# Feed-forward gradients with the hidden index as adjacent rows of w_down per partition, and products that contract the four batch rows

## The chip, the cores and the metric

The kernel runs on one core of a Trainium2 chip. The metric is the device time of one execution in microseconds (us). Each kernel was executed several times; the text gives medians, and beside them ratios to the kernel before. A program on one core also has faster and slower executions. "Clock" is the TensorE clock that the throttle granted, as a share of full speed.

## The reference, cut to what matters

The reference computes one decode step of a parallel attention and feed-forward block, and all its gradients.

```python
# B = 4 batch rows, S = 1, D = 512, F = 1792; 32 query heads, 8 KV heads, Sk = 4096, Dh = 128, bf16
def _A_ref(x, k_cache, v_cache, wq, wo):     # attention over the last W = 1024 keys
    ...
def _B_ref(x, w_gate, w_up, w_down):
    return (_gelu(x @ w_gate) * (x @ w_up)) @ w_down

xn = _layernorm(x)
out = x + _A_ref(xn, ...) + _B_ref(xn, ...)
# returned: out, and the gradients of x, k_cache, v_cache, wq, wo, w_gate, w_up, w_down
```

The gradients of the caches are zero outside the last 1024 keys, so the kernel also stores about 50 MB of zeros. The gradients of the three feed-forward weights are outer products summed over only four batch rows.

## The kernel before

Four parts matter. First, w_down is loaded so that hidden index f = c*128 + p: partition p holds the rows p, 128+p and so on, in packets of 1 KB.

```python
for c0 in range(0, NF, NF // 2):                       # NF = 14
    nc.sync.dma_start(out=wd_sb[:, c0:c0 + NF // 2, :],
                      in_=B_w_down[c0 * P:(c0 + NF // 2) * P, :].rearrange("(c p) n -> p c n", p=P))
```

Second, the feed-forward reads its weights in columns that lie side by side, and its masks are made on GpSimd.

```python
nc.tensor.matmul(h_ps[:, fc, :], lhsT=wsb[:, c, fc * P:(fc + 1) * P], rhs=xnT[:, c, :], ...)   # hg, hu
...
for src, dst in ((dy_b, dym), (xn_b, xnm)):
    for i in range(rep):
        nc.gpsimd.tensor_scalar(out=dst[:, i, :], in0=src[:], scalar1=msk_i[:, i:i + 1], ...)
```

Third, the weight gradients. The activations are turned into rows, four blocks of 128 hidden units in 4 rows per batch row; a product takes all 128 partitions, and the mask leaves four that are not zero. They run in the background of attention: each "tick" of the attention code starts one.

```python
def piece_d(f4, i, n, held):                           # gradient of w_down, 14 of these
    mps = ps_w.tile([P, D], FP32, name="dwd_ps", tag="w")
    nc.tensor.matmul(mps[:], lhsT=a_r[:, f4, :], rhs=dym[:, i, :], start=True, stop=True)
    ...
def piece_g(s_r, og, c, i, held):                      # gradients of w_gate and w_up, 32 of these
    n = (NF - i + 3) // 4                              # 4 or 3 blocks: 512 or 384 columns
    mps = ps_w.tile([P, NF4, P], FP32, name="dwg_ps", tag="w")
    nc.tensor.matmul(mps[:, 0:n, :].rearrange("p f d -> p (f d)"), lhsT=xnm[:, i, c:D:ND],
                     rhs=s_r[:, 0:n, :].rearrange("p f d -> p (f d)"), start=True, stop=True)
    evac(held["osb"][:, 0:n, i, :], mps[:, 0:n, :], n * P)
```

Fourth, attention runs in four steps t. Each step's gradients of V and K go through staging tiles, of which there are three; zeros are queued by ScalarE at fixed places (`zeros(4 if t >= NT - 2 else 0)` is one).

## Time and profile before

| | before |
|---|---|
| median of the first three runs | 284.48 us |
| span of the profiled run | 281.7 us |
| mean granted clock | 0.896 |
| TensorE busy | 210.1 us, 75% |
| DMA | 112.15 MB, mean 398 GB/s |

In a table of windows the columns are: stretch, its length, busy us (and instructions) of TensorE's matmuls, TensorE's weight loads, VectorE, ScalarE and GpSimd, then granted clock, DMA share, GB/s.

### The profile page before, as it was taken

The page shows a single profiled execution, that of the slowest core. Times are in us where ns is not written, and L with a number is a line of the kernel's source. Part 1 is how long each engine was busy: PE and PEld are TensorE (multiplying, and loading weights), DVE is VectorE, ACT ScalarE, POOL GpSimd, SP SyncE. Part 2 cuts the span into 40 slices and gives each one's busy share as a digit, 9 for nine tenths or more (in the row PEclk, how much of TensorE's full clock was granted, in tenths as well). Part 3 has the DMA queues.
Part 4 walks back from the last instruction along what each step waited for, and adds up shares of the span by engine and source line. Part 5 has one row for each costly group of instructions (what it writes and reads, how often), then busy time and mean ns, then how long its engine had stood idle before and what let it go on. Part 6 is the DMA issues. An engine that isn't in the chain of part 4 may idle for free.

```text
span 281.7 us, 7190 instructions
## 1 busy us (share of the span) xinstructions
PE 210.1 (75%) x3132; PEld 135.9 (48%) x3132; DVE 158.7 (56%) x336; ACT 115.6 (41%) x214; POOL 56.0 (20%) x56
## 2 busy tenths in 40 slices
PE   1968976968769699967793399786963996878950
PEld 0856854634536465534461265454641654526520
DVE  6945754626467457645672137547651465367691
ACT  1421743344535146535421335435502563571540
POOL 3890003400200633020024060110050201002000
PEclk9975999979988989999999559979995999799795
DMA  7999999999999999999999969999999779999995
GB/s 236 445 398 426 423 405 413 408 418 419 422 427 426 420 425 417 425 422 425 428 420 409 406 202 347 425 426 426 416 427 429 318 301 409 428 427 423 419 416 221
DMA packets 19407, 112.15 MB, mean 398 GB/s; under 512 B 1440, under 2 KB 5040, under 8 KB 10416
## 3 DMA queue, kind: packets, MB, share of 16 engines
q10 hardware_dynamic: 4384, 50.34, 42.4%
q1 hardware_dynamic: 12304, 44.58, 39.1%
q0 software_dynamic: 2688, 16.78, 15.1%
q8 instruction: 24, 0.39, 0.5%
q14 instruction: 7, 0.06, 0.0%
HBM read 30.68 MB, written 81.01 MB: 396 GB/s over the span
## 4 chain that ended last, share of the span: by engine, by line
PE 45%; DMA 27%; DVE 16%; ACT 4%; issue 3%; POOL 2%; ACTq 0%; DVEq 0%; SPq 0%
DMA out_dram<-stg_dv 18%; PE T_ps L399 10%; PE kv_ps L537 8%; PE S_ps L404 6%; DMA out_dram<-osb_d 6%; DVE T_sb L101 4%; DMA out_dram<-ztile 4%; PE dwo_ps L556 3%; PE acc_ps L213 3%; PE dwq_ps L568 2%; POOL P_x L417 2%; PE wqT_ps L595 2%; PE wgT_ps L742 2%; PE od_ps L509 1%; PE dwg_ps L715 1%
## 5 line engine op out<-in xcount | busy, mean ns | idle before, releaser
L101 DVE COPY T_sb<-T_ps 128x1024 bf16<-128x1024 bf16 x64 | 43.8, 691 | 41.2 <-PE T_ps L399 40.8
L99 ACT CAST stg_dk<-kv_ps 128x512 bf16<-128x512 f32 x40 | 22.2, 589 | 54.0 <-PE kv_ps L537 36.0
L99 ACT CAST stg_dv<-kv_ps 128x512 bf16<-128x512 f32 x57 | 30.4, 593 | 30.0 <-PE kv_ps L537 30.0
L537 PE MATMUL kv_ps<-qmr,dS_x 128*128 128x512 bf16 x64 | 22.9, 448 | 16.9 <-ACT stg_dk L99 15.3
L537 PE MATMUL kv_ps<-domr,P_x 128*128 128x512 bf16 x64 | 22.8, 427 | 5.4 <-POOL P_x L417 4.8
L101 DVE CAST stg_dk<-kv_ps 128x512 bf16<-128x512 f32 x24 | 16.1, 686 | 17.8 <-PE kv_ps L537 17.6
L399 PEld LDWEIGHTS <-kb 128*128 128x128 bf16 x256 | 18.6, 105 | 10.7 <-issue 7.8
L399 PE MATMUL T_ps<-ident,kb 128*128 128x128 bf16 x256 | 23.4, 231 | 0.0
L386 POOL TENSOR_TENSOR domr<-r,msk 128x512 bf16<-128x512 bf16 x8 | 8.2, 1040 | 71.2 <-DVE r L379 71.2
L99 ACT CAST osb_g<-dwg_ps 128x512 bf16<-128x512 f32 (+1 forms) x28 | 14.1, 540 | 18.4 <-PE dwg_ps L715 11.5
L399 PE MATMUL T_ps<-ident,vb 128*128 128x128 bf16 x256 | 21.3, 226 | 0.0
L399 PEld LDWEIGHTS <-vb 128*128 128x128 bf16 x256 | 16.6, 102 | 6.9 <-issue 5.0
L417 POOL TENSOR_TENSOR P_x<-P_b,bmsk 128x1024 bf16<-128x1024 bf16 x4 | 7.6, 1894 | 56.3 <-ACT P_b L465 56.3
L404 PE MATMUL S_ps<-T_sb,dom 128*32 128x256 bf16 x128 | 12.7, 387 | 8.0 <-DVE T_sb L101 7.5
L99 ACT CAST osb_o<-dwo_ps 128x512 bf16<-128x512 f32 x25 | 14.5, 587 | 9.3 <-PE dwo_ps L556 8.5
L99 ACT CAST osb_q<-dwq_ps 128x512 bf16<-128x512 f32 x25 | 14.3, 588 | 8.4 <-PE dwq_ps L568 7.8
L595 PEld LDWEIGHTS <-wq_sb 128*128 128x128 bf16 x128 | 9.0, 103 | 16.7 <-issue 15.1
L101 DVE COPY woT<-woT_ps 128x1024 bf16<-128x1024 bf16 x16 | 11.0, 689 | 8.8 <-PE woT_ps L338 8.8
L101 DVE COPY wqT<-wqT_ps 128x1024 bf16<-128x1024 bf16 x16 | 11.0, 689 | 5.6 <-PE wqT_ps L595 5.5
L101 DVE COPY wgT<-wgT_ps 128x1024 bf16<-128x1024 bf16 x14 | 9.7, 692 | 7.2 <-PE wgT_ps L742 7.2
L595 PE MATMUL wqT_ps<-ident,wq_sb 128*128 128x128 bf16 x128 | 11.1, 230 | 3.5 <-issue 3.1
L556 PE MATMUL dwo_ps<-dyz,od_x 128*128 128x512 bf16 x32 | 13.4, 453 | 0.2 <-ACT osb_o L99 0.2
(214 smaller groups left out, 392.1 us busy)
## 6 DMA issues: line engine op xcount, KB each, us to landing
out_dram<-ztile ACTq DMA_DIRECT2D x15, 3072.0 KB, 18.9
out_dram<-stg_dv SPq DMA_DIRECT2D x8, 1024.0 KB, 20.0
out_dram<-stg_dk SPq DMA_DIRECT2D x8, 1024.0 KB, 13.1
kb<-in_A_k_cache_dram POOLq DMA_DIRECT2D x5, 1024.0 KB, 18.3
vb<-in_A_v_cache_dram POOLq DMA_DIRECT2D x5, 1024.0 KB, 25.4
out_dram<-osb_o SPq DMA_DIRECT2D x8, 512.0 KB, 14.7
out_dram<-osb_q SPq DMA_DIRECT2D x8, 512.0 KB, 16.7
out_dram<-osb_g SPq DMA_DIRECT2D x8, 448.0 KB, 15.2
```

The source lines that it names most:

```text
L99: last.append(nc.scalar.copy(out=out, in_=in_))
L101: return nc.vector.tensor_copy(out=out, in_=in_)
L213: nc.tensor.matmul(ps[:, c, :], lhsT=lf(c), rhs=rhs, start=(k == 0), stop=(k == len(terms) - 1))
L386: nc.gpsimd.tensor_tensor(out=mr[:, g], in0=st[t]["r4"][:, k, :].unsqueeze(1).broadcast_to([P, NQ, Dh]), in1=msk[:, :, g].unsqueeze(2).bro ...
L399: nc.tensor.transpose(T_ps[:, jj, :], blks[(t, g)][:, q * JQ + jj, :], ident[:])
L404: nc.tensor.matmul(ps[b * RG:(b + 1) * RG, :], lhsT=lf[:, b, s * RG:(s + 1) * RG], rhs=T_sb[:, :, b], start=(g == 0 and q == 0), stop=(g = ...
L417: eng.tensor_tensor(out=dst[:].rearrange("p j (m b) -> p (j m) b", b=B), in0=src[:].unsqueeze(2).broadcast_to([P, WQ, B]), in1=bmsk[:].uns ...
L537: nc.tensor.matmul(mps[:].rearrange("p q d -> p (q d)"), lhsT=src[:, jj, :], rhs=mr[:, g].rearrange("p q d -> p (q d)"), start=True, stop= ...
L556: nc.tensor.matmul(mps[:], lhsT=X[:].rearrange("p h d -> p (h d)")[:, g * rep + i:CW:HG], rhs=dyz[:], start=True, stop=True)
L568: nc.tensor.matmul(mps[:], lhsT=xnz[:, c:D:ND], rhs=X[:, g * rep:(g + 1) * rep, :].rearrange("p i d -> p (i d)"), start=True, stop=True)
L595: nc.tensor.transpose(wT_ps[:, i, c, :], wq_sb[:, c, h * Dh:(h + 1) * Dh], ident[:])
L742: nc.tensor.transpose(wT_ps[:, i, c, :], wsb[:, c, fc * P:(fc + 1) * P], ident[:])
```

## The change

The intent: let partition p own 14 adjacent rows of w_down, f = p*14 + c. Then each half of w_down is loaded in packets of 7 KB and its gradient stored in packets of 4 KB and 2 KB. The products contract the four batch rows themselves, so the eight GpSimd masks go. Five of the 64 units of zeros move into the attention steps where DMA had dips. The price: the columns of w_gate and w_up that belong to one c lie 28 bytes apart, and the columns of their gradients have to come out in the order p, c, which the moving operand of dwg_ps restores by reading f_r with a step of 256 bytes.

```diff
-                      in_=B_w_down[c0 * P:(c0 + NF // 2) * P, :].rearrange("(c p) n -> p c n", p=P))
+                      in_=B_w_down.rearrange("(p c) n -> p c n", p=P)[:, c0:c0 + NF // 2, :])
...
-    for src, dst in ((dy_b, dym), (xn_b, xnm)):        # eight masked copies on GpSimd
-        ...
...                                                     # a staging tile of dV or dK begins
+                    if (k, g) == (1, GP - 1) and 0 < t < NT - 1:
+                        zeros(2 if t == 1 else 3)
...                                                     # hg, hu and, alike, the transposes of w_gate, w_up
-  lhsT=wsb[:, c, fc * P:(fc + 1) * P], rhs=xnT[:, c, :]
+  lhsT=wsb[:, c, fc:F:NF], rhs=xnT[:, c, :]
...
+    f_r = const.tile([P, NF, P], BF16, name="f_r")     # rows 0-3: a, 32-35: dhg, 64-67: dhu
...
-        nc.tensor.matmul(mps[:], lhsT=a_r[:, f4, :], rhs=dym[:, i, :], start=True, stop=True)
+        nc.tensor.matmul(mps[:], lhsT=f_r[0:B, 4 * f4 + i, :], rhs=dy_b[0:B, :], start=True, stop=True)
...
-        nc.tensor.matmul(mps[:, 0:n, :].rearrange("p f d -> p (f d)"), lhsT=xnm[:, i, c:D:ND],
-                         rhs=s_r[:, 0:n, :].rearrange("p f d -> p (f d)"), start=True, stop=True)
+        nc.tensor.matmul(mps[:], lhsT=xn_b[r0:r0 + B, c:D:ND],
+                         rhs=f_r[r0:r0 + B, :, i * PC:(i + 1) * PC].rearrange("b c p -> b p c"), start=True, stop=True,
+                         tile_position=(r0, 0))
...
-            zeros(4 if t >= NT - 2 else 0)
+            zeros({NT - 2: 2, NT - 1: 1}.get(t, 0))
```

All 32 dwg_ps products now have 448 columns; before, 16 had 512 and 16 had 384. The replicated copies of x_n and dy also change from "batch, repeat" to "repeat, batch" rows, so that rows r0 to r0+3 are the four batch rows.

More of the change, by code (lines that the diff above doesn't have):

```diff
@@ L132 @@
     RB = P // B
-    spread = ffn.tile([B, B, RB], BF16, name="spread")
-    nc.vector.tensor_copy(out=spread[:], in_=ident[0:B, 0:B].unsqueeze(2).broadcast_to([B, B, RB]))
+    spread = ffn.tile([B, RB, B], BF16, name="spread")
+    nc.vector.tensor_copy(out=spread[:], in_=ident[0:B, 0:B].unsqueeze(1).broadcast_to([B, RB, B]))
     dy_b = const.tile([P, D], BF16, name="dy_b")
@@ L138 @@
         b_ps = ps_w.tile([P, D], FP32, name="b_ps", tag="w")
-        nc.tensor.matmul(b_ps[:], lhsT=spread[:].rearrange("k b r -> k (b r)"), rhs=src[:], start=True, stop=True)
+        nc.tensor.matmul(b_ps[:], lhsT=spread[:].rearrange("k r b -> k (r b)"), rhs=src[:], start=True, stop=True)
         nc.vector.tensor_copy(out=dst[:], in_=b_ps[:])
@@ L144 @@
     nc.vector.memset(one_f[:], 1.0)
-    msk_i = const.tile([P, rep], FP32, name="msk_i")
-    nc.vector.reduce_sum(out=msk_i[:], in_=ident_f[:].rearrange("p (b r) -> p r b", b=B)[:, 0:rep, :], axis=AX.X)
     hmsk_f = const.tile([P, GP, B * rep], FP32, name="hmsk_f")
@@ L167 @@
         nc.vector.tensor_copy(out=sel[:, :, b * rep:(b + 1) * rep],
-                              in_=ident_f[:, b * RB:b * RB + 1].unsqueeze(2).broadcast_to([P, 2 * GP, rep]))
+                              in_=ident_f[:, b:b + 1].unsqueeze(2).broadcast_to([P, 2 * GP, rep]))
     sc_od = const.tile([P, 1], FP32, name="sc_od")
@@ L241 @@
             nc.tensor.transpose(tps[:, c, :], src[:, c:D:ND] if adj else src[:, c * P:(c + 1) * P], ident[:])
-        nc.vector.tensor_copy(out=dstT[:], in_=tps[:].rearrange("p c (b r) -> p c b r", b=B)[:, :, :, 0])
+        nc.vector.tensor_copy(out=dstT[:], in_=tps[:, :, 0:B])
         if src is dy_b:
@@ L246 @@
             nc.vector.tensor_copy(out=dyT8[:].rearrange("p c (b r) -> p c b r", b=B),
-                                  in_=tps[:].rearrange("p c (b r) -> p c b r", b=B)[:, :, :, 0:8])
-    xnm = const.tile([P, rep, D], BF16, name="xnm")
-    dym = ffn.tile([P, rep, D], BF16, name="dym")
-    for src, dst in ((dy_b, dym), (xn_b, xnm)):
-        for i in range(rep):
-            nc.gpsimd.tensor_scalar(out=dst[:, i, :], in0=src[:], scalar1=msk_i[:, i:i + 1], scalar2=None,
-                                    op0=ALU.mult)
+                                  in_=tps[:].rearrange("p c (r b) -> p c b r", b=B)[:, :, :, 0:8])
     dyz = const.tile([P, D], BF16, name="dyz")
@@ L620, in ftb @@
     def ftb(name):
-        t_ = ffn.tile([P, 4 * NF4, B], BF16, name=name)
-        nc.vector.memset(t_[:], 0.0)
-        return t_
+        return ffn.tile([P, NF, B], BF16, name=name)
     da_ps = ps_a.tile([P, NF, B], FP32, name="da_ps", tag="dP")
@@ L642, in up @@
             for c in range(ND):
-                nc.tensor.matmul(h_ps[:, fc, :], lhsT=wsb[:, c, fc * P:(fc + 1) * P], rhs=xnT[:, c, :],
+                nc.tensor.matmul(h_ps[:, fc, :], lhsT=wsb[:, c, fc:F:NF], rhs=xnT[:, c, :],
                                  start=(c == 0), stop=(c == ND - 1))
@@ L676 @@
     aT_b = ftb("aT_b")
-    nc.vector.tensor_tensor(out=aT_b[:, 0:NF, :], in0=gl[:], in1=hu, op=ALU.mult)
+    nc.vector.tensor_tensor(out=aT_b[:], in0=gl[:], in1=hu, op=ALU.mult)
     dhuT_b = ftb("dhuT_b")
-    nc.vector.tensor_tensor(out=dhuT_b[:, 0:NF, :], in0=da[:], in1=gl[:], op=ALU.mult)
+    nc.vector.tensor_tensor(out=dhuT_b[:], in0=da[:], in1=gl[:], op=ALU.mult)
     dhg_f = ft("dhg_f")
@@ L682, with f_rows @@
     dhgT_b = ftb("dhgT_b")
-    nc.vector.tensor_tensor(out=dhgT_b[:, 0:NF, :], in0=dhg_f[:], in1=gp[:], op=ALU.mult)
+    nc.vector.tensor_tensor(out=dhgT_b[:], in0=dhg_f[:], in1=gp[:], op=ALU.mult)
     acc_sum(0, [(lambda c, fc=fc: wd_sb[:, fc, c * P:(c + 1) * P], aT_b[:, fc, :]) for fc in range(NF)])
-    def f_rows(srcT, nm):
-        ps = od_ps[:]
-        for f4 in range(NF4):
-            for b in range(B):
-                nc.tensor.matmul(ps[b * RB:b * RB + 4, f4, :], lhsT=srcT[:, 4 * f4:4 * f4 + 4, b], rhs=ident[:],
-                                 start=True, stop=True, tile_position=(0, b * RB))
-        rows = const.tile([P, NF4, P], BF16, name=nm)
-        evac(rows[:], ps, 512)
-        return rows
-    a_r = f_rows(aT_b, "a_r")
+    f_r = const.tile([P, NF, P], BF16, name="f_r")
+    def f_rows(srcT, r0):
+        for f0 in range(0, NF, 4):
+            n = min(4, NF - f0)
+            ps = ps_w.tile([P, 4, P], FP32, name="fr_ps", tag="w")
+            for i in range(n):
+                nc.tensor.matmul(ps[r0:r0 + B, i, :], lhsT=srcT[:, f0 + i, :], rhs=ident[:], start=True, stop=True,
+                                 tile_position=(0, r0))
+            evac(f_r[r0:r0 + B, f0:f0 + n, :], ps[r0:r0 + B, 0:n, :], n * P)
+    f_rows(aT_b, 0)
     def piece_d(f4, i, n, held):
@@ L702, in piece_d, with piece_g @@
         mps = ps_w.tile([P, D], FP32, name="dwd_ps", tag="w")
-        nc.tensor.matmul(mps[:], lhsT=a_r[:, f4, :], rhs=dym[:, i, :], start=True, stop=True)
+        nc.tensor.matmul(mps[:], lhsT=f_r[0:B, 4 * f4 + i, :], rhs=dy_b[0:B, :], start=True, stop=True)
         evac(held["osb"][:, i, :], mps[:], 512)
         if i == n - 1:
-            store(nc.sync, out=out_8[4 * f4 * P:(4 * f4 + n) * P, :].rearrange("(h p) n -> p h n", p=P),
+            store(nc.sync, out=out_8.rearrange("(p c) n -> p c n", p=P)[:, 4 * f4:4 * f4 + n, :],
                                 in_=held["osb"][:, 0:n, :], kind="rest",
                       apart=["zeros", "rest"])
-    def piece_g(s_r, og, c, i, held):
+    PC = P // 4
+    def piece_g(r0, og, c, i, held):
         if i == 0:
-            held["osb"] = outp.tile([P, NF4, 4, P], BF16, name="osb_g", tag="o")
-        n = (NF - i + 3) // 4
-        mps = ps_w.tile([P, NF4, P], FP32, name="dwg_ps", tag="w")
-        nc.tensor.matmul(mps[:, 0:n, :].rearrange("p f d -> p (f d)"), lhsT=xnm[:, i, c:D:ND],
-                         rhs=s_r[:, 0:n, :].rearrange("p f d -> p (f d)"), start=True, stop=True)
-        evac(held["osb"][:, 0:n, i, :], mps[:, 0:n, :], n * P)
+            held["osb"] = outp.tile([P, 4, PC, NF], BF16, name="osb_g", tag="o")
+        mps = ps_w.tile([P, PC, NF], FP32, name="dwg_ps", tag="w")
+        nc.tensor.matmul(mps[:], lhsT=xn_b[r0:r0 + B, c:D:ND],
+                         rhs=f_r[r0:r0 + B, :, i * PC:(i + 1) * PC].rearrange("b c p -> b p c"), start=True, stop=True,
+                         tile_position=(r0, 0))
+        evac(held["osb"][:, i], mps[:], NF * PC)
         if i == 3:
             store(nc.sync, out=og.rearrange("(p c) f -> p c f", c=ND)[:, c, :],
-                                in_=held["osb"][:].rearrange("p f i d -> p (f i d)")[:, 0:F], kind="rest",
+                                in_=held["osb"][:].rearrange("p i x c -> p (i x c)"), kind="rest",
                       apart=["zeros", "rest"])
@@ L730 @@
     nc.tensor.matmul(df_ps[:].rearrange("p c b -> p (c b)"), start=True, stop=False, **edge)
-    for srcT, wsb, og, nm in ((dhgT_b, wg_sb, out_6, "dhg_r"), (dhuT_b, wu_sb, out_7, "dhu_r")):
-        s_r = f_rows(srcT, nm)
+    for srcT, wsb, og, r0 in ((dhgT_b, wg_sb, out_6, 32), (dhuT_b, wu_sb, out_7, 64)):
+        f_rows(srcT, r0)
         for c in range(ND):
@@ L735 @@
             for i in range(4):
-                bg.append(lambda s_r=s_r, og=og, c=c, i=i, held=held: piece_g(s_r, og, c, i, held))
+                bg.append(lambda r0=r0, og=og, c=c, i=i, held=held: piece_g(r0, og, c, i, held))
         for f2 in range(NF // 2):
@@ L741 @@
                 for c in range(ND):
-                    nc.tensor.transpose(wT_ps[:, i, c, :], wsb[:, c, fc * P:(fc + 1) * P], ident[:])
+                    nc.tensor.transpose(wT_ps[:, i, c, :], wsb[:, c, fc:F:NF], ident[:])
             wgT = tsb.tile([P, 2, ND, P], BF16, name="wgT", tag="wT")
@@ L786 @@
         zeros(2 * B * G)
-        acc_r = kvp.tile([P, 2, ND, B, RB], FP32, name="acc_r", tag="kb")
-        nc.vector.tensor_copy(out=acc_r[:], in_=acc[:].unsqueeze(4).broadcast_to([P, 2, ND, B, RB]))
+        acc_r = kvp.tile([P, 2, ND, RB, B], FP32, name="acc_r", tag="kb")
+        nc.vector.tensor_copy(out=acc_r[:], in_=acc[:].unsqueeze(3).broadcast_to([P, 2, ND, RB, B]))
         fin_ps = []
@@ L794 @@
             for c in range(ND):
-                nc.tensor.transpose(f_ps[:, c, :], acc_r[:, o, c].rearrange("p b r -> p (b r)"), ident_f[:])
+                nc.tensor.transpose(f_ps[:, c, :], acc_r[:, o, c].rearrange("p r b -> p (r b)"), ident_f[:])
             fin_ps.append(f_ps[:])
@@ L803 @@
         nc.vector.tensor_tensor(out=out_b[:], in0=acc_o, in1=x_b[:], op=ALU.add)
-        nc.sync.dma_start(out=out_0.rearrange("b s d -> (b s) d"), in_=out_b[0:P:RB, :])
+        nc.sync.dma_start(out=out_0.rearrange("b s d -> (b s) d"), in_=out_b[0:B, :])
         s1 = const.tile([P, 1], FP32, name="s1")
@@ L821 @@
         nc.vector.tensor_tensor(out=dx_b[:], in0=pr[:], in1=dy_b[:], op=ALU.add)
-        nc.sync.dma_start(out=out_1.rearrange("b s d -> (b s) d"), in_=dx_b[0:P:RB, :])
+        nc.sync.dma_start(out=out_1.rearrange("b s d -> (b s) d"), in_=dx_b[0:B, :])
 _INS = ['A_x', 'A_k_cache', 'A_v_cache', 'A_wq', 'A_wo', 'B_x', 'B_w_gate', 'B_w_up', 'B_w_down', 'grad_out']
```

## The prediction

> **What bounds the kernel now.** I read the page first: engine shares, then the 40 slices, then the chain that ended last; then a table of 3 us windows, the waits, and the groups by shape.
>
> ```profile
> PE 210.1 (75%) x3132; PEld 135.9 (48%) x3132; DVE 158.7 (56%) x336; ACT 115.6 (41%) x214; POOL 56.0 (20%) x56
> ...
> DMA  7999999999999999999999969999999779999995
> GB/s 236 445 398 426 423 405 413 408 418 419 422 427 426 420 425 417 425 422 425 428 420 409 406 202 347 425 426 426 416 427 429 318 301 409 428 427 423 419 416 221
> DMA packets 19407, 112.15 MB, mean 398 GB/s; under 512 B 1440, under 2 KB 5040, under 8 KB 10416
> ```
>
> No compute engine is full, but the DMA row is 9 almost everywhere. 112.15 MB at the 420 GB/s of the full slices is 267 us, out of a span of 281.7. About 15 us are left: the start, two dips (slices 23-24 and 31-32), the tail, and slices a few per cent slow. The windows size the dips (columns: stretch, its length, the five engines' busy us and instructions, clock, DMA share, GB/s).
>
> ```profile
> 159.00:162.00 3.00, 2.71 (x19) 1.76 (x18) 1.38 (x2) 1.97 (x5) 0.00 (x0) 0.50 0.89 377
> 162.00:165.00 3.00, 2.71 (x69) 2.11 (x69) 0.84 (x4) 0.32 (x1) 1.34 (x3) 0.50 0.31 85
> 165.00:168.00 3.00, 3.00 (x24) 2.00 (x23) 1.77 (x3) 1.49 (x3) 3.00 (x4) 0.50 0.83 318
> 168.00:171.00 3.00, 3.00 (x32) 1.71 (x32) 1.36 (x2) 2.03 (x4) 0.10 (x1) 0.95 0.89 183
> ...
> 219.00:222.00 3.00, 2.71 (x78) 2.39 (x78) 0.66 (x4) 0.94 (x3) 0.01 (x1) 0.91 0.91 380
> 222.00:225.00 3.00, 3.00 (x35) 1.67 (x33) 1.85 (x4) 1.92 (x4) 2.03 (x2) 1.00 0.55 229
> 225.00:228.00 3.00, 3.00 (x37) 1.94 (x35) 2.59 (x4) 1.56 (x3) 0.00 (x0) 1.00 0.87 347
> 228.00:231.00 3.00, 3.00 (x34) 1.56 (x32) 1.92 (x4) 2.25 (x5) 0.00 (x0) 1.00 0.47 188
> ```
>
> First dip: (43+335+102+237) GB/s below 420, times 3 us, is 2.15 MB, or 5.1 us. Second: (40+191+73+232) x 3 = 1.61 MB, 3.8 us. Together 8.9 us. Their cause is in the chain (start, length, what):
>
> ```profile
> 131.30 27.25 DMA out_dram<-stg_dv
> ...
> 191.32 24.14 DMA out_dram<-stg_dv
> ```
>
> A dV store waits 24 to 27 us behind other traffic. The fourth staging tile of a step (dK, second head) reuses the buffer of the first dV tile, of three, so ScalarE stands until that store lands, and TensorE behind it:
>
> ```profile
> ACT stg_dk L99 <- DMA out_dram<-stg_dv: 17.8, 3, 9.5
> ```
>
> Meanwhile the queues run dry, since the next loads and stores come from compute that stands. After 215.46 us, where the second such store lands, the chain holds no DMA: 60 us of plain compute to dx_b at 275.6 us, then 6.1 us in which the last stores drain. So the bound alternates: DMA to 158 us, compute a little, DMA to 215 us, compute to the end.
>
> **What the Trainium skill says.** "DMA: Bandwidth & Descriptors", section "Why small descriptors are slow (HBM only)": each packet has a fixed overhead. The trace's packet records agree: a 1 KB packet takes 47.9 ns on its engine, 2 KB 84.8, 4 KB 160, 8 KB 312; per byte, 1 KB costs 1.2 times 4 KB. Same page, "Queues, rings and completion order": each engine goes round the queues packet by packet. The trace agrees: while ScalarE's 12 KB zero packets wait, the SyncE queue with 2 KB packets gets only about 50 to 60 GB/s of 425 (132 to 141 us). "TensorE: Matmul & The Clock Gate", section "LDWEIGHTS (loading the stationary operand)": a load costs its columns, not its rows. A product over 4 rows should thus cost what one over 128 does; before, the two 4-row b_ps products of 512 columns took 602 and 629 ns and the slowest 128-row product of 512 columns (dwd_ps) 634. "Advanced Engine Details and Errata", "SBUF Cachelines": a new 16-byte line at every access is slower. The trace agrees for weights: in oT_ps (step 16 bytes) loads follow one another every 60 ns, in hg_ps (contiguous) every 26.
>
> **The change part by part.**
> Packets. w_down's load goes from 1792 packets of 1 KB to 256 of 7 KB. 1792 x 47.9 / 16 engines = 5.4 us; 7 KB at some 273 ns (between 4 and 8 KB), x 256 / 16 = 4.4 us. Saved 1.0. Its gradient's stores go from 1792 of 1 KB to 384 of 4 KB and 128 of 2 KB: 5.4 to 4.5 us, saved 0.9. Sum -1.9 us of DMA work, in a stretch where DMA is full, so it should show in the landing of the first dV store.
>
> Masks. GpSimd loses eight products:
>
> ```profile
> L254 POOL TENSOR_SCALAR dym<-dy_b,msk_i 128x512 bf16<-128x512 bf16 x4 | 6.4, 1614 | 5.2 <-DVE hmsk_f L152 5.2
> L254 POOL TENSOR_SCALAR xnm<-xn_b,msk_i 128x512 bf16<-128x512 bf16 x4 | 6.2, 1558 | 0.0
> ```
>
> 12.6 us of an engine 20% busy, never on the chain then: 0 by themselves. Perhaps 1 us comes from VectorE, whose xn_f took 942 ns beside them and whose like (pr, L818) takes 546 alone.
>
> Added compute. hg and hu now load w_gate and w_up with a step of 28 bytes: 112 loads at about 60 instead of 26 ns, +3.8 us on the feed-forward chain; the transposes of the same matrices go at 56 ns anyway, so +0.5. Row extraction has 12 evacuations instead of 3, 9 x 0.59 = 5.3 us over two engines, of which perhaps 1 us is on the path. The 32 dW_gate and dW_up products read their moving operand with a step of 256 bytes:
>
> ```profile
> L715 PE MATMUL dwg_ps<-dhu_r,xnm 128*128 128x512 bf16 x8 | 3.0, 415 | 0.0
> ```
>
> The scores (step 8 bytes, 256 columns) take 387 ns where contiguous 512 columns take 379: such reads run at about half speed. I choose +0.2 to +0.6 us each, 6 to 19 us of TensorE time in step 0, mostly in its idle slots. So compute reaches the 149 us point some 4 to 8 us later, less some of a 3.8 us wait for an osb_d store, which lands sooner. ScalarE waits 9.5 us there, so all or nearly all is hidden; I charge 2 us, for DMA queues that may run thin near 40 us.
>
> Zeros. A unit is 64 x 12 KB = 0.786 MB, 1.9 us at 420 GB/s; 64 units in both. The change takes 2 units from the end of step 2's scores and 3 from step 3's, and puts 2 in front of the fourth staging tile of step 1 (149 us) and 3 there in step 2 (208 us). They are 3.7 and 5.6 us, aimed at dips of 5.1 and 3.8. They are issued before the wait, not in it, so part only lengthens the wait. I count 55% of 8.9 us, about -5 us, to be seen as shorter dips and, since 5 units fewer remain for the last 90 us, a shorter tail.
>
> Sum: -1.9 - 5 + 2 + 0.5 (rounding the small TensorE terms up) = -4.4 us. 284.5 - 4.4 = 280.1, say 280.0.
>
> **The rivals.**
> 1. The zeros delay the very store that is waited for. For: 12 KB packets beat the other queues, and the store has 9 us to go when they are queued. Then the dip only shifts by up to 3.7 us, and compute after it too; with the packets' 1.9 us the time is 283 to 286. Against: the queue still held zeros at 149 us, so new ones go behind them.
> 2. Compute becomes the bound of step 0. For: strided loads and 256-byte moving reads, on an engine busy 75%. If it arrives over 9.5 us late, or the queues run dry near 40 and 65 us, each microsecond counts: 285 to 290. Against: the slack named.
> 3. The gain is hidden: DMA ends earlier but the last 60 us are compute, which does not shorten. Then only the tail falls, by at most the 3 us or so that the last stores stand in line: 281 to 283.
> 4. All fits: both dips filled, tail shorter, 274 to 277.
>
> **Range and chances.** Centre 280.0. Low 275.0 (rival 4), high 286.0 (rivals 1 and 2 in part). The 2% line is 278.8: faster 0.36, since filling three quarters of the dips is enough; slower (over 290.2) needs rival 2 in full, 0.06; within 2%, 0.58.
>
> **What would show it.** Packets: about 16,600 instead of 19,407, those under 2 KB from 5040 to some 1456; w_down halves landing sooner than 5.4 us. Zeros: GB/s over 380 throughout the stretches after the two dV landings; if rival 1 holds, the wait of stg_dk for stg_dv grows beyond 17.8 us. Compute: hg's and hu's weight loads every 60 ns, dwg_ps products of 550 to 1000 ns; if rival 2 holds, that wait vanishes and dips appear before 80 us. Tail: last store landing within 4 us of dx_b. The prediction is wrong if the compute cost of the strides is over 9 us, or if the dips move and do not shrink.

## More of the kernel before

The slices of the page cut the span in 40 parts. One digit is a tenth: 9 in the PE row is 90% busy or more, and in the PEclk row it is 90% of full clock.

```profile
PE   1968976968769699967793399786963996878950
PEclk9975999979988989999999559979995999799795
```

The clock is at half in the fourth slice, then mostly high until TensorE stands still near 155 and 215 us. The trace's clock records begin only at 11.3 us; the page shows what lies before them as full clock.

In the groups, the second number after the bar is the mean time of one instruction in ns:

```profile
L703 PE MATMUL dwd_ps<-dym,a_r 128*128 128x512 bf16 x14 | 5.8, 413 | 0.0
L715 PE MATMUL dwg_ps<-dhg_r,xnm 128*128 128x512 bf16 x8 | 2.8, 386 | 0.0
L643 PE MATMUL hg_ps<-xnT,wg_sb 128*128 128x4 bf16 x56 | 1.6, 165 | 0.8 <-DVE xnz L265 0.8
```

```profile
18.00:48.00 30.00, 24.71 (x530) 19.82 (x527) 16.11 (x38) 11.04 (x20) 5.45 (x6) 0.83 1.03 413
48.00:78.00 30.00, 24.31 (x289) 15.30 (x287) 15.40 (x31) 14.41 (x31) 5.93 (x5) 0.94 1.01 418
78.00:108.00 30.00, 24.38 (x424) 15.16 (x424) 17.97 (x37) 12.20 (x23) 7.89 (x10) 0.89 1.01 423
```

The reader is to see the DMA share: it is full in all three.

## The result

The changed kernel took **312.14 us** (median of 4, 310.60 to 314.83), the kernel before 284.39 beside it. The ratio is 1.0989, with a 95% interval of 1.0904 to 1.1075: slower. All ratios here are the mean time of one kernel's fast runs over that of the other's of the same rounds, so not quite the ratio of the medians. Where a ratio is turned into us below, ratio minus one is multiplied by 284.4; for the change that is +28.1.

The page of the changed kernel, the rows that answer to those shown of before:

```profile
span 309.4 us, 7172 instructions
...
PE 254.3 (82%) x3126; PEld 152.9 (49%) x3126; DVE 162.0 (52%) x337; ACT 118.0 (38%) x218; POOL 43.3 (14%) x48
...
PE   2978989999999889899679949967179699697781
PEclk9965995555555589989996975999659969999877
DMA  7999863998499597799999999999999876999984
GB/s 292 428 388 419 345 273 87 381 423 342 186 427 418 226 417 315 268 337 402 424 430 426 414 426 388 418 425 426 432 421 424 354 299 265 422 413 418 415 334 149
DMA packets 16623, 112.15 MB, mean 362 GB/s; under 512 B 1472, under 2 KB 1488, under 8 KB 7632
```

From slice 7 to 14 the clock is at half while the PE row is at 9 or close to it. The DMA row has holes from slice 5 on, where it had none before. The same windows as before:

```profile
18.00:48.00 30.00, 27.13 (x393) 22.15 (x392) 14.16 (x36) 9.93 (x18) 0.00 (x0) 0.73 0.83 334
48.00:78.00 30.00, 30.00 (x247) 13.40 (x246) 10.46 (x20) 8.95 (x17) 6.59 (x8) 0.50 0.81 318
78.00:108.00 30.00, 29.22 (x152) 12.50 (x152) 10.10 (x19) 8.84 (x18) 1.89 (x1) 0.50 0.78 324
```

TensorE's records cover 59.22 of these last 60 us, against 48.69 before, and yet it finished fewer instructions, 399 against 713. DMA moved less in each of the three: (413-334 + 418-318 + 423-324) GB/s x 30 us = 8.3 MB, at 420 GB/s 20 us of DMA time. That is most of the loss. The groups:

```profile
L707 PE MATMUL dwg_ps<-f_r,xn_b 4*128 4x448 bf16 x32 | 28.4, 918 | 0.0
L693 PE MATMUL dwd_ps<-dy_b,f_r 4*128 4x512 bf16 x14 | 6.5, 462 | 0.0
L631 PE MATMUL hg_ps<-xnT,wg_sb 128*128 128x4 bf16 x56 | 3.5, 199 | 0.8 <-DVE xnz L253 0.8
```

Where the loss arises is told by when stores were issued, in us from the start:

| issue of | before | after | later by |
|---|---|---|---|
| first store of dW_down | 30.48 | 35.62 | 5.1 |
| last store of dW_down | 42.48 | 52.31 | 9.8 |
| last store of dW_up | 77.43 | 107.70 | 30.3 |
| first dV store, step 0 | 86.55 | 114.89 | 28.3 |
| first dV store, step 1 | 131.30 | 158.43 | 27.1 |
| first dV store, step 2 | 191.32 | 213.88 | 22.6 |
| first dV store, step 3 | 247.04 | 275.37 | 28.3 |

All of it is there by 108 us, when the last background product ends. Some 5.7 us are then won back by step 2, since ScalarE no longer waits long for the dV store, and they are lost again by step 3, in a wait that was not there before:

```profile
ACT stg_dk L99 <- DMA out_dram<-stg_dv: 5.2, 2, 3.2
...
PE woT_ps L326 <- DMA wo_sb<-in_A_wo_dram: 7.8, 1, 7.8
```

The first line was 17.8 us before. The second is new: the load of w_o for step 3 was issued last of its step's loads on GpSimd's queue, after those of w_q and of the caches, where before it came first. It took from 187.04 to 223.08 us to land (before: 163.66 to 169.01).

### The profile page after: what moved, and what is told of

Its sections match the earlier page's. It is cut to its first block, busy times and chain, and to the rows that moved or that the text cites. A ratio compares the mean times of both kernels' runs of the same rounds, so it can differ in the third digit from the quotient of the medians.

```text
span 309.4 us, 7172 instructions
## 1 busy us (share of the span) xinstructions
PE 254.3 (82%) x3126; PEld 152.9 (49%) x3126; DVE 162.0 (52%) x337; ACT 118.0 (38%) x218; POOL 43.3 (14%) x48
## 2 busy tenths in 40 slices
DMA packets 16623, 112.15 MB, mean 362 GB/s; under 512 B 1472, under 2 KB 1488, under 8 KB 7632
## 4 chain that ended last, share of the span: by engine, by line
PE 57%; DMA 23%; DVE 13%; ACT 2%; issue 2%; POOL 1%; ACTq 0%; DVEq 0%
DMA out_dram<-stg_dv 12%; DMA wo_sb<-in_A_wo_dram 12%; PE T_ps L387 10%; PE dwg_ps L707 9%; PE kv_ps L527 7%; PE S_ps L392 4%; PE wgT_ps L735 3%; PE woT_ps L326 3%; PE acc_ps L209 3%; PE dwo_ps L546 2%; DVE T_sb L101 2%; PE wqT_ps L585 2%; PE dwd_ps L693 2%; POOL P_x L405 1%; PE df_ps L740 1%
## 5 line engine op out<-in xcount | busy, mean ns | idle before, releaser
L99 ACT CAST osb_g<-dwg_ps 128x448 bf16<-128x448 f32 x28 | 14.9, 531 | 36.9 <-PE dwg_ps L707 36.9
L707 PE MATMUL dwg_ps<-f_r,xn_b 4*128 4x448 bf16 x32 | 28.4, 918 | 0.0
L387 PE MATMUL T_ps<-ident,kb 128*128 128x128 bf16 x256 | 27.7, 257 | 0.0
L387 PEld LDWEIGHTS <-kb 128*128 128x128 bf16 x256 | 21.0, 116 | 12.9 <-issue 10.9
L387 PE MATMUL T_ps<-ident,vb 128*128 128x128 bf16 x256 | 24.0, 243 | 0.0
L387 PEld LDWEIGHTS <-vb 128*128 128x128 bf16 x256 | 18.1, 109 | 11.5 <-issue 9.7
L326 PE MATMUL woT_ps<-ident,wo_sb 128*128 128x128 bf16 x128 | 14.2, 271 | 8.8 <-DMA wo_sb<-in_A_wo_dram 7.8
L326 PEld LDWEIGHTS <-wo_sb 128*128 128x128 bf16 x128 | 11.2, 123 | 15.8 <-DMA wo_sb<-in_A_wo_dram 8.1
L99 ACT CAST osb_q<-dwq_ps 128x512 bf16<-128x512 f32 x23 | 13.2, 586 | 8.6 <-PE dwq_ps L558 8.1
L546 PE MATMUL dwo_ps<-dyz,od_x 128*128 128x512 bf16 x32 | 14.3, 494 | 0.0
## 6 DMA issues: line engine op xcount, KB each, us to landing
kb<-in_A_k_cache_dram POOLq DMA_DIRECT2D x5, 1024.0 KB, 19.3
```

The lines of the kernel that those rows point to most:

```text
L99: last.append(nc.scalar.copy(out=out, in_=in_))
L326: nc.tensor.transpose(wT_ps[:, i, c, :], wo_sb[:, 2 * h2 + i, c * P:(c + 1) * P], ident[:])
L387: nc.tensor.transpose(T_ps[:, jj, :], blks[(t, g)][:, q * JQ + jj, :], ident[:])
L546: nc.tensor.matmul(mps[:], lhsT=X[:].rearrange("p h d -> p (h d)")[:, g * rep + i:CW:HG], rhs=dyz[:], start=True, stop=True)
L707: nc.tensor.matmul(mps[:], lhsT=xn_b[r0:r0 + B, c:D:ND], rhs=f_r[r0:r0 + B, :, i * PC:(i + 1) * PC].rearrange("b c p -> b p c"), start=Tru ...
```

## The experiments

The two theories at the start: **A**, the read with the 256-byte step costs the time; **B**, products that contract only four rows leave the clock at half, whatever they read. Smaller suspects: the stepped weights, and the zeros with w_o's place. A kernel that is wrong on purpose has wrong gradients and nothing else changed in its flow.

### e1: contiguous moving read, still four rows

```diff
-    f_r = const.tile([P, NF, P], BF16, name="f_r")
+    f_r = const.tile([P, P, NF], BF16, name="f_r")
-            evac(f_r[r0:r0 + B, f0:f0 + n, :], ps[r0:r0 + B, 0:n, :], n * P)
+            evac(f_r[r0:r0 + B, :, f0:f0 + n].rearrange("b p c -> b c p"), ps[r0:r0 + B, 0:n, :], n * P)
...                                                     # dwd_ps: its stationary operand becomes f_r[0:B, :, 4 * f4 + i]
-      rhs=f_r[r0:r0 + B, :, i * PC:(i + 1) * PC].rearrange("b c p -> b p c")
+      rhs=f_r[r0:r0 + B, i * PC:(i + 1) * PC, :]
```

> The changed kernel with f_r stored index-last, so that the 32 dW_gate and dW_up products read their moving operand contiguously; they still contract 4 rows. Theory A (the 256-byte step of the moving operand is the cost): dwg_ps products fall from 918 ns to some 350 to 400, the TensorE clock is near full from 48 to 108 us, time 284 to 292 us. Theory B (products over 4 rows leave TensorE at half clock, whatever they read): the clock stays at 0.50 through step 0, dwg_ps products 540 to 640 ns, time over 298 us.

Measured: correct, 314.63 us, ratio 1.1048 [1.0995, 1.1100]. dwg_ps fell from 918 to 560 ns, and the clock stayed at half. That is as B has it, but the run is not clean: the evacuations into f_r now write every 28 bytes, and 4 partitions of 512 elements took 2480 ns on ScalarE instead of 576. The stationary operand of dwd_ps has that step as well now. This cost arises early, so the time says little about the read.

### e2: the stepped read alone, in the kernel before (wrong)

```diff
-                         rhs=s_r[:, 0:n, :].rearrange("p f d -> p (f d)"), start=True, stop=True)
+                         rhs=s_r[:, 0:n, :].rearrange("p f d -> p d f"), start=True, stop=True)
```

> The kernel before with one edit: the same 32 products read their moving operand with a step of 256 bytes, still over 128 rows with masks (gradients of w_gate and w_up are wrong on purpose). Theory A: dwg_ps products 800 to 1000 ns, clock at half in step 0, time 300 to 312 us. Theory B: clock stays as before, products longer by at most 250 ns, time 284 to 291 us.

Measured: 292.29 us, ratio 1.0255 [1.0205, 1.0305], or +7.3 us.

```profile
L715 PE MATMUL dwg_ps<-dhg_r,xnm 128*128 128x512 bf16 x8 | 8.0, 1041 | 0.0
```

With 128 rows, 512 columns took 1041 ns in place of 386. Neither expectation held whole: the products grew by more than B's 250 ns, and the clock in 48 to 78 us fell to 0.73 (before: 0.94) but not to half. Theory A is a real cost, but a quarter of the loss. The step is that of the change, the pattern is not quite: four or three blocks in a row here, 14 in the changed kernel. That is 2.03 ns a column for 512 columns and 1.46 for 384, against 2.05 there.

### e3: the zeros at their old places

```diff
-                    if (k, g) == (1, GP - 1) and 0 < t < NT - 1:
-                        zeros(2 if t == 1 else 3)
-            zeros({NT - 2: 2, NT - 1: 1}.get(t, 0))
+            zeros(4 if t >= NT - 2 else 0)
```

> The changed kernel with the zero stores where the kernel before has them; this also brings back the old order of step 3's loads (w_o first). If the moved zeros and that order cost time, 304 to 309 us and no wait of woT_ps for w_o; if they help or are neutral, 311 to 316 us.

Measured: correct, 307.57 us, ratio 1.0745 [1.0684, 1.0807], or +21.2 us. With the zeros, w_o's load went back to the front of its queue, and the wait of 7.8 us was gone. So the move that was to win 5 us cost the changed kernel 5.3 (by medians of the fast runs) to 6.9 us (by ratios). Which share is the zeros' own and which is the load order's is not separated.

### e5: the new index alone, with masks, 128 rows and contiguous read

```diff
-  (w_down's load and store, the weights' columns: as in the change)
-            held["osb"] = outp.tile([P, NF4, 4, P], BF16, name="osb_g", tag="o")
+            held["osb"] = outp.tile([P, P, NF], BF16, name="osb_g", tag="o")
-        evac(held["osb"][:, 0:n, i, :], mps[:, 0:n, :], n * P)
+        evac(held["osb"][:, :, i:NF:4].rearrange("p d f -> p f d"), mps[:, 0:n, :], n * P)
```

> The kernel before with the feed-forward index as adjacent rows of w_down alone (7 KB loads, 4 KB stores, strided weight loads of w_gate and w_up), masks and 128-row products kept, moving operand contiguous, the order restored in the evacuations' writes. Both theories: no half clock in step 0, time 282 to 288 us. If the index itself (strided weight loads) carries the loss: over 295 us.

Measured: correct, 307.40 us, ratio 1.0788 [1.0743, 1.0834]. The expectation missed, and the profile says why:

```profile
L99 ACT CAST osb_g<-dwg_ps 128x512 bf16<-128x512 f32 x15 | 35.3, 2583 | 1.4 <-issue 1.3
```

The order was restored by the evacuation, which writes bf16 elements in steps of 28 bytes: 2583 ns in place of 587. ScalarE became the bound of step 0. The clock fell too, to 0.68 in 48 to 78 us and 0.56 in 78 to 108 us, with all 128 rows but with TensorE busy for 19.93 and 21.72 of 30 us only: few rows are not the only thing that comes with a low clock. The run does not say what the index costs, but it shows that this is not the way to restore an order.

### e6: 128 rows in the changed kernel, the stepped read kept

The tile f_r is filled with zeros first, and the other operand is a copy that is zero outside its own four rows. Results stay correct.

```diff
+    nc.gpsimd.memset(f_r[:], 0.0)
+    for r0, src, nm in ((0, dy_b, "dy_m"), (32, xn_b, "xn_g"), (64, xn_b, "xn_u")):
+        fmsk[r0] = const.tile([P, D], BF16, name=nm)
+        nc.gpsimd.memset(fmsk[r0][:], 0.0)
+        nc.gpsimd.tensor_copy(out=fmsk[r0][r0:r0 + B, :], in_=src[r0:r0 + B, :])
-        nc.tensor.matmul(mps[:], lhsT=f_r[0:B, 4 * f4 + i, :], rhs=dy_b[0:B, :], start=True, stop=True)
+        nc.tensor.matmul(mps[:], lhsT=f_r[:, 4 * f4 + i, :], rhs=fmsk[0][:], start=True, stop=True)
-        nc.tensor.matmul(mps[:], lhsT=xn_b[r0:r0 + B, c:D:ND], rhs=f_r[r0:r0 + B, ...], ..., tile_position=(r0, 0))
+        nc.tensor.matmul(mps[:], lhsT=fmsk[r0][:, c:D:ND], rhs=f_r[:, ...], ...)
```

> The changed kernel with its dW products contracting all 128 rows again: f_r is filled with zeros first, and the other operand is a copy (of x_n twice, of dy once) that is zero outside its own four rows, so the results stay correct. The moving read still has the 256-byte step. Theory B (four-row products hold the clock at half from 48 to 108 us, whatever they read): the granted clock in 48 to 108 us goes back above 0.75, dwg_ps from 918 to some 520 ns or less, span 293 to 301 us. Theory A (the stepped read alone costs the time, the row count is harmless): clock stays 0.50 there, dwg_ps stays near 918 ns, span 307 to 315 us.

Measured: correct, 296.88 us, ratio 1.0445 [1.0387, 1.0502]: 15 us less than the changed kernel, for a change that adds nothing but rows of zeros.

```profile
PEclk9965899589987998899959859979569779999777
...
48.00:78.00 30.00, 29.97 (x264) 12.69 (x262) 12.44 (x25) 10.33 (x20) 5.68 (x7) 0.83 0.98 386
78.00:108.00 30.00, 28.16 (x330) 14.21 (x333) 16.25 (x33) 13.12 (x27) 1.90 (x1) 0.89 0.99 409
```

The clock is back, as B has it. B's second number was wrong: dwg_ps stayed at 923 and 920 ns. So the stepped product takes its 0.92 us at either clock, and what the low clock had cost must lie in the work between those products. Since the added rows hold zeros only, their values need not be other than zero to bring the clock back.

### e9: four rows alone, in the kernel before (wrong)

```diff
-        nc.tensor.matmul(mps[:], lhsT=a_r[:, f4, :], rhs=dym[:, i, :], ...)
+        nc.tensor.matmul(mps[:], lhsT=a_r[0:4, f4, :], rhs=dym[0:4, i, :], ...)
-      lhsT=xnm[:, i, c:D:ND], rhs=s_r[:, 0:n, :]
+      lhsT=xnm[0:4, i, c:D:ND], rhs=s_r[0:4, 0:n, :]
```

> The kernel before, where dwd_ps and dwg_ps contract rows 0 to 3 alone (wrong outputs for the three weight gradients, on purpose); everything else as before. Theory B: the clock in 48 to 86 us falls to 0.50, dwg_ps goes from 336-415 to 500-640 ns, span 289 to 298. Theory A: clock as before (above 0.8 from 48 to 86 us), span 283 to 286.

Measured: 300.77 us, ratio 1.0542 [1.0471, 1.0613], or +15.4 us, at the upper end of what B expected (spans of the fast runs 297.3, 297.6 and 300.4 us).

```profile
PEclk9965555555555569999987966997998599799895
```

```profile
L715 PE MATMUL dwg_ps<-dhg_r,xnm 4*128 4x512 bf16 x8 | 4.5, 611 | 0.0
```

Nothing was changed but the rows read. The clock, which rises from half at some 28 us in the kernel before, now stays at half until about 109 us. This is the largest single cost of the change.

### e7: contiguous read through PSUM, still four rows

The order is restored where the rows are made: 56 products of 32 columns write index-last into PSUM, so that evacuation and read are both contiguous. Only dhg and dhu go this way.

```diff
+        for j in range(4):
+            ps = ps_w.tile([P, P // 4, NF], FP32, name="fn_ps", tag="w")
+            for f in range(NF):
+                nc.tensor.matmul(ps[r0:r0 + B, :, f], lhsT=srcT[:, f, :], rhs=ident[:, j * 32:(j + 1) * 32], ...)
+            evac(f_n[r0:r0 + B, j * 32:(j + 1) * 32, :], ps[r0:r0 + B, :, :], NF * 32)
```

> The changed kernel with the order of the index restored in PSUM: the row extraction for dhg and dhu writes its products index-last into PSUM (32 columns each, 56 products instead of 14), so that the evacuation and the moving read of dwg_ps are both contiguous; still four rows; correct. It repeats the first experiment without its slow evacuations. Theory A (stepped read): dwg_ps from 918 to 250 to 400 ns, clock in 48 to 108 us above 0.75, span 290 to 302. Theory B (four rows keep the clock at half): dwg_ps 450 to 640 ns, clock stays near 0.50 there, span 300 to 310.

Measured: correct, 307.05 us (median of 5 runs); ratio 1.0772 [1.0718, 1.0827], or +22.0 us. Its profiled run was slow, so its details count for less; dwg_ps took 561 ns there and the clock in 48 to 78 us was 0.50. This is e1 without its flaw: the stepped read is worth some 5 to 6 us in the changed kernel, and the clock stays low without it.

### e11: the zeros' new places, in the kernel before

```diff
+                    if (k, g) == (1, GP - 1) and 0 < t < NT - 1:
+                        zeros(2 if t == 1 else 3)
-            zeros(4 if t >= NT - 2 else 0)
+            zeros({NT - 2: 2, NT - 1: 1}.get(t, 0))
```

> The kernel before with only the zeros moved to the places of the change (two units at step 1, three at step 2, fewer at the end). The prediction's step: -5 us, so 279 to 281. Its rival 1, and the reading of the run with the old places of the zeros (where moving them back saved some 4.5 us): the zeros lengthen the wait for the dV store and push step 3's w_o load to the end of its queue, 285 to 290.

Measured: correct, 283.71 us, ratio 0.9958 [0.9915, 1.0001], or -1.2 us with an interval that touches zero, so neither the -5 us nor the loss that was expected. Here are the two dips in windows, e11 first, the kernel before second:

```profile
159.00:171.00 12.00, 8.84 (x111) 6.21 (x110) 3.99 (x8) 4.53 (x9) 4.41 (x6) 0.50 1.02 405
...
222.00:237.00 15.00, 14.47 (x141) 8.35 (x139) 8.72 (x17) 7.59 (x14) 2.04 (x2) 0.86 0.67 277
```

```profile
159.00:171.00 12.00, 11.43 (x139) 7.57 (x138) 5.36 (x10) 5.81 (x11) 4.44 (x6) 0.61 0.73 241
...
222.00:237.00 15.00, 13.96 (x152) 8.22 (x150) 9.75 (x18) 8.75 (x17) 2.03 (x2) 1.00 0.79 326
```

The first dip was filled, from 241 to 405 GB/s. The second was not; it came later and deeper, 277 in place of 326 GB/s (over 210 to 240 us, which holds the whole dip in both, 350 in place of 372). The first gain was handed back there and in the tail. The wait of ScalarE for a dV store, 17.8 us before, grew a little, which is the sign that rival 1 of the prediction had named:

```profile
ACT stg_dk L99 <- DMA out_dram<-stg_dv: 19.3, 3, 11.2
```

The load of w_o for step 3 was issued last here too and took 26.1 us to land, but TensorE did not wait for it. So its place in the queue need not cost time by itself.

### e8: the stepped weights alone, in the kernel before (wrong)

```diff
-  wsb[:, c, fc * P:(fc + 1) * P]       # in hg, hu and in the transposes of w_gate and w_up
+  wsb[:, c, fc:F:NF]
```

> The kernel before with only the weights of hg, hu and of the w_gate/w_up transposes read with the 28-byte step (wrong outputs on purpose). The prediction's step: 112 loads at 60 instead of 26 ns, +3.8 us on the feed-forward chain, nearly all hidden later: hg and hu 3.4 to 3.5 us instead of 1.6 each, span 284 to 287 us. Rival: the later start of step 0 is not hidden, 288 to 291.

Measured: 288.24 us, ratio 1.0095 [1.0046, 1.0145], or +2.7 us. hg and hu took 3.5 us each in place of 1.6, as expected. The first store of dW_down went out 3.7 us later and the first dV store of step 0 6.7 us later; part of it was won back afterwards. The time is in the range of the rival: the later start is not hidden.

### e12 and e13: both repairs, and both with the old zeros

These are e6 and e7 together (all three sources go through PSUM), e13 with the zeros of e3 besides. The products become:

```diff
-  lhsT=f_r[0:B, 4 * f4 + i, :], rhs=dy_b[0:B, :]                                   # dwd_ps
+  lhsT=f_n[:, :, 4 * f4 + i], rhs=fmsk[0][:]
-  lhsT=xn_b[r0:r0 + B, c:D:ND], rhs=f_r[r0:r0 + B, :, i * PC:(i + 1) * PC].rearrange("b c p -> b p c")
+  lhsT=fmsk[r0][:, c:D:ND], rhs=f_n[:, i * PC:(i + 1) * PC, :]                      # dwg_ps
```

> The changed kernel with both repairs: all 128 rows contracted (zero-filled f_r, masked other operand) and the order of the index restored in PSUM, so the moving read of dwg_ps is contiguous. Correct. What stays of the change: the 7 KB and 4 KB packets, the stepped weight loads of hg, hu and w_gate/w_up transposes, the moved zeros and w_o's place. If row count and stepped read together are the loss: dwg_ps 330 to 420 ns, clock above 0.8 in 48 to 108 us, span 286 to 292 us (some 7 us, the price of the step in the kernel before, below the 297 of the run with 128 rows). If the stepped weights or the load order matter more than I think: 293 to 298.

> The same as the run with both repairs, but with the zeros at their old places, so w_o comes first on its queue again. If the 4.5 us that the old places saved in the changed kernel are theirs alone: 282 to 287 us, 3 to 5 below the run with both repairs. If the zeros matter only to a kernel that is late (they gave -1.2 us in the kernel before): within 2 us of that run. A time below 281 would make it the best version.

Measured, both correct: e12 294.48 us, ratio 1.0313 [1.0272, 1.0355]; e13 292.57 us, ratio 1.0240 [1.0192, 1.0288]. dwg_ps took 360 ns, and the clock was 1.00 in 48 to 78 us and 0.94 (e12) and 0.89 (e13) after that. So the two repairs restore what they were to restore, yet e12 is in the slower of its two expected ranges, and e13 is still 6.8 us slower than before. Stepped weights are 2.7 of these. The first store of dW_down went out at 37.06 us in e13, 2.9 later than in e8; the extraction in 56 small products per source is the likely reason, but no run takes it away alone. The old zeros were worth 2 us here.

### e15 and e18: 64 and 96 rows, in the kernel before (wrong)

They are e9 with more rows:

```diff
-  lhsT=xnm[:, i, c:D:ND], rhs=s_r[:, 0:n, :]
+  lhsT=xnm[0:64, i, c:D:ND], rhs=s_r[0:64, 0:n, :]       # e15; 0:96 in e18; dwd_ps alike
```

> The kernel before, where dwd_ps and dwg_ps contract rows 0 to 63 (wrong on purpose), to see whether the clock follows the number of rows or only tells few from many. If it follows the share of rows in use: clock in 48 to 86 us between 0.50 and 0.94, span between 286 and 298 us. If half the rows are enough: clock as before, 283 to 286 us.

> The kernel before, where dwd_ps and dwg_ps contract rows 0 to 95 (wrong on purpose). If the clock needs (nearly) all rows: 0.50 in 48 to 78 us, dwg_ps about 610 ns for 512 columns, 292 to 302 us. If more than half the rows are enough: dwg_ps 390 to 450 ns, 284 to 288 us.

Measured: 64 rows 299.06 us, ratio of the fast runs 1.0380 [1.0287, 1.0472] (two of its four runs counted as slow, at 300 and 301 us); 96 rows 285.81 us, ratio 1.0031 [0.9973, 1.0089]. A group and a window of each, 64 rows first:

```profile
L715 PE MATMUL dwg_ps<-dhg_r,xnm 64*128 64x512 bf16 x8 | 4.5, 616 | 0.0
...
48.00:78.00 30.00, 28.17 (x263) 15.08 (x261) 11.89 (x22) 9.29 (x18) 6.63 (x8) 0.50 0.87 340
```

```profile
L715 PE MATMUL dwg_ps<-dhg_r,xnm 96*128 96x512 bf16 x8 | 2.8, 386 | 0.6 <-ACT osb_g L99 0.6
...
48.00:78.00 30.00, 24.96 (x302) 15.54 (x292) 15.60 (x31) 14.26 (x31) 5.92 (x5) 0.94 1.02 419
```

With 64 rows the products are as slow as with four, 616 against 611 ns, and the clock in 48 to 78 us is 0.50. So half the rows are not enough, and the clock does not follow their share. With 96 rows they take the 386 ns of 128. In this stretch it is a step between 64 and 96 rows, not a slope; where in between was not tried. With 64 rows the clock came back somewhat earlier, 0.65 in 78 to 108 us against 0.50 with four.

### e19: only the 14 dwd_ps products with four rows (wrong)

```diff
-  lhsT=a_r[:, f4, :], rhs=dym[:, i, :]
+  lhsT=a_r[0:4, f4, :], rhs=dym[0:4, i, :]
```

> The kernel before, where only the 14 dwd_ps products contract 4 rows and the 32 dwg_ps products all 128 (wrong w_down gradient on purpose). If a low clock between 27 and 42 us is what costs, since it delays everything after: +4 to +8, so 288 to 293 us. If the clock recovers at once after the last of them and the delay is absorbed: 284 to 287.

Measured: 292.46 us, ratio 1.0301 [1.0251, 1.0352], or +8.6 us.

```profile
PEclk9975555569999987999959859979996799999796
```

The low clock, at its half in slice 4 too in the kernel before, lasts into slice 9, to some 63 us, and is normal after that. The last store of dW_down went out 8.75 us later (51.23 against 42.48), the first dV store of step 0 8.4, that of step 3 7.8, and the end came 8.6 later. Here an early delay goes through to the end nearly one to one.

### e20: the three costs together, in the kernel before (wrong)

It is e2, e8 and e9 in one kernel; packets, masks, extraction and zeros are those of before.

```diff
-  lhsT=xnm[:, i, c:D:ND], rhs=s_r[:, 0:n, :].rearrange("p f d -> p (f d)")
+  lhsT=xnm[0:4, i, c:D:ND], rhs=s_r[0:4, 0:n, :].rearrange("p f d -> p d f")
-  lhsT=a_r[:, f4, :], rhs=dym[:, i, :]
+  lhsT=a_r[0:4, f4, :], rhs=dym[0:4, i, :]
-  wsb[:, c, fc * P:(fc + 1) * P]
+  wsb[:, c, fc:F:NF]
```

> The kernel before with the three suspected costs together: dW products contract 4 rows, dwg_ps reads its moving operand with the 256-byte step, hg, hu and the w_gate/w_up transposes read their weights with the 28-byte step (wrong outputs on purpose). Packets, masks, zeros and row extraction are those of before. If the three are the whole loss and add up: +15.4 +7.2 +2.7 = 25 us, so 308 to 313. If they overlap (the products are slow once, whether by clock or by step): 300 to 307, and the rest of the 28 us comes from the zeros and w_o's place.

Measured: 312.57 us, ratio 1.0968 [1.0896, 1.1039], or +27.5 us. The single costs sum to 15.4 + 7.3 + 2.7 = 25.4.

```profile
PEclk9965555555555557999999985997998579899895
...
GB/s 260 441 399 421 335 246 92 254 417 410 157 423 418 320 411 187 202 383 359 429 425 426 423 419 355 325 426 426 428 416 426 427 210 335 411 424 420 423 415 241
```

The clock row and the holes of the changed kernel are here without the zeros' move and without the new packets. The three costs make up a loss as large as the whole, and within the noise they add (the interval is about 2 us to either side for e9 and e20, 1.4 for e2 and e8).

### e16: only the first part of the zeros' move, in the kernel before

```diff
+                    if (k, g) == (1, GP - 1) and t == 1:
+                        zeros(2)
-            zeros(4 if t >= NT - 2 else 0)
+            zeros({NT - 2: 2, NT - 1: 4}.get(t, 0))
```

> The kernel before with only the first part of the zeros' move: two units in front of the fourth staging tile of step 1, none at step 2, two and four at the last two steps. If filling the first dip (5.1 us of DMA time) without pushing the second is worth something: 279 to 283 us, ratio below 0.99. If the last 60 us of compute set the end whatever is filled: ratio 0.992 to 1.002.

Measured: correct, 284.85 us, ratio 0.9974 [0.9916, 1.0033]: no difference shown. None of the versions tried beats the kernel before beyond doubt.

## Why the prediction was wrong

**What failed most: "A product over 4 rows should thus cost what one over 128 does."** This step of the prediction took its evidence from three durations, 602 and 629 ns with four rows and 634 ns for "the slowest 128-row product". The slowest was the wrong one to take: it was the first of its group, at 26.0 us, in a stretch with a clock of 0.50, and the median of the group was 379 ns. The two 4-row products ran at 6 us, before the clock records begin, so the full clock that the page shows there is not measured; in e9 such products took 602 ns at a clock of 0.50. All three were thus probably durations at half clock. Compared at one clock, the sentence is true for a single product: in the changed kernel the 14 dwd_ps products with four rows had a minimum of 384 and a median of 386 ns, most of them at full clock. What was not asked is what such products do to the clock itself. Four rows alone cost 15.4 us (e9), and giving the rows back wins 15 us (e6). The prediction had put this at zero.

**The stepped read: size right, hiding wrong.** The prediction chose "+0.2 to +0.6 us each, 6 to 19 us", and e2 shows +0.65 us for 512 columns and some +0.2 for 384 (559 against 336 to 372 ns), 7.3 us in the total. It had compute arrive "some 4 to 8 us later" and charged only 2 us for this and the rest of the added compute, because ScalarE waits 9.5 us later on. With the lost clock it arrived 27.1 us later (first dV store of step 1). That wait did absorb something: it fell from 17.8 to 5.2 us in all. But DMA was full from 18 to 108 us, and loads and stores that are issued late leave holes that cannot be filled later; e19 and e8 show that a delay of the first 50 us arrives at the end, almost whole (8.75 us and 8.6) or in part (6.7 us at step 0 and 2.7).

**The stepped weights.** "60 instead of 26 ns" was right: 3.48 us for 56 loads and products is 62 ns each (29 before, counted alike). "Nearly all is hidden" was not: +2.7 us alone (e8).

**Zeros: "about -5 us".** The first dip was filled as said, the second was not, and the net was -1.2 us (e11), nothing that the interval separates from zero. In the changed kernel the move cost 5.3 to 6.9 us, with w_o's load at the end of its queue (e3). The prediction did not look at the order of the loads. Its rival 1 spoke of zeros that delay a store: that showed in e11 (17.8 to 19.3 us), while in the changed kernel the wait that was new was one for a load.

**Packets and masks.** The counts were right: 16,623 packets against "about 16,600", under 2 KB 1488 against "some 1456", and the halves of w_down landed in 4.8 and 6.5 us, rather than 5.4 each (4.7 each in e3 and e13). Their worth was not measured alone. The one hint is e3 (+21.2), which has them and the three costs, against e20 (+27.5), which has only the costs: 6.3 us in favour of the rest of the change, not separated further, and with other column counts and read patterns per product.

**The balance.** Three costs +27.5, the rest of the change -6.3, the zeros and w_o's place +6.9: +28.1. The last two terms are differences of the same runs, so the sum closes by construction; what is independent is the first term.

**The rivals.** Rival 2 named what happened, compute as the bound of step 0, and both its signs came: the long wait nearly vanished, and dips appeared before 80 us. But it was sized at 285 to 290, and a time above 290.2, which it would have to cause "in full", was given 6%: its sum lacked the clock. The prediction's last sentence, "wrong if the compute cost of the strides is over 9 us", was met as well, if not clearly: 7.3 + 2.7 = 10.0, each known to 1.4 us or so.

**What stays open.** The clock is not low whenever few-row products run: in the changed kernel it was 1.00 from 33 to 45 us while four-row dwd_ps products ran among transposes, fell in 45 to 48 us, and then stayed at half. In e19 the same 14 products held it down from the start. What it is in a product of at most 64 rows that goes with a low clock, the rows in use or another way in which such a product is run, no run separates. How often such products must come, and where between 64 and 96 rows the step lies, was not tried. Nor is it settled why e13, with everything repaired but the weights, is 4.1 us slower than e8.

## What to carry to other kernels

Before narrowing a product to the rows that matter, ask what it does to the granted clock: here rows of zeros won 15 us (e6) and leaving rows out cost 15 us (e9), so look at the clock row and not only at one product's duration. Put the reordering of an index neither in a stepped evacuation nor in a stepped moving operand without measuring it; each took 2.7 to 4.4 times as long as the contiguous form for 512 columns. And where DMA is full, do not count a later wait as slack for an early delay: test it, as a delay in the first 50 us came out at the end almost whole in e19 and in part in e8.

## What the Trainium skill lacked or had wrong

- "TensorE: Matmul & The Clock Gate", "Part 1: The HAM clock gate (the "warmup" mystery)" says that the gate follows how busy TensorE has been. Here it was busy for 30.00 of 30 us by its records (48 to 78 us, changed kernel) at a clock of 0.50. The page lacks that rows count: in that stretch 0.50 with 4 and with 64 rows in the dW products, 0.94 with 96 and 128 (e9, e15, e18, kernel before), and the added rows may be zeros (e6: 0.83).
- The same page, "Why this matters for your kernels", has a single product with K=32 cost the time of one with K=128. That holds for one product at full clock (medians 386 with 4 rows, 379 with 128, 512 columns), but in a kernel full of such products it misleads: 611 against 386 ns for 4 rows in e9, and +15.4 us.
- "Advanced Engine Details and Errata", "SBUF Cachelines" speaks of a penalty without a size. Moving operand with a 256-byte step: 1041 against 386 ns (512 columns). Stationary operand with a 28-byte step: 62 against 29 ns per load and product of hg. bf16 writes with a 28-byte step: ScalarE 2583 against 587 ns (128 x 512), and 2480 against 576 with only 4 partitions.
- No page has it that a stepped moving read can be indifferent to the clock: 918 to 923 ns for 448 columns at 0.50 and at 0.83 to 0.89.
